# One new order for all operations of an attention and feed-forward kernel

## The chip, the cores and the metric

The program runs on one NeuronCore of a Trainium2 chip. The metric is the device time of one execution in microseconds, lower is better; the time of a kernel is the median of its runs. A profile is one further execution, recorded by the hardware profiler, with a time of its own.

The core has five queues of instructions: PE (matrix products), DVE (element-wise work), ACT (element-wise work and functions such as exp), POOL (slower element-wise work) and SP (which here only starts transfers). Each takes its instructions strictly in order; an instruction that has to wait holds up all that stand behind it on the same engine. Transfers run on 16 DMA engines. In this kernel SP and ACT start them.

## The reference

```python
def rmsnorm(x, g):
    rms = np.sqrt(np.mean(x * x, axis=-1, keepdims=True) + 1e-06)
    return x / rms * g
# q, k, v: (8 batches, 12 heads, 448 positions, 64); float32
q_n, k_n = rmsnorm(q, g_q), rmsnorm(k, g_k)
attn = softmax(q_n @ k_n^T / sqrt(64))
x = (attn @ v), heads side by side             # 3584 x 768
out = ((x @ w_a) * (x @ w_b)) @ w_out           # 768 -> 1536 -> 768
```

The three weight matrices arrive as float64; all else is float32.

## The kernel before

**Two halves of work.** Attention goes over 24 groups `p` of four heads (three groups per batch, 8 batches). The feed-forward part goes over four pairs of batches, `beta` 0 to 3.

**Attention of one group.** SP loads q, k and v. ACT squares q and k (`squares`, L424), DVE adds the squares up (L426), POOL takes the power -1/2 (L432), DVE scales q (`apply`, qn, L436). PE transposes k and q (`transposes`, L462) and ACT copies both out of PSUM (qkT: L467 for k, L469 for q). For each of seven blocks `j`, PE makes the scores (`scores`, sc, L483), ACT the exponentials (ET, L489), PE the products with v (`values`, o, L505). The sums of the exponentials are made on PE with a matrix of ones for the first five groups (`sums_over_keys`, su, L541), later on DVE and POOL. Then `invert`: ACT copies the sums (rec, L554), SP spreads one row over many partitions (few, L561), DVE takes the reciprocal (L574), SP writes it to DRAM and reads it back to all partitions (L566, L570), DVE multiplies (`divide`, L612). The tiles that hold scores (tag `sc`) are two in number, so the third score product waits for the exponentials of the first.

**Weights.** 18 pieces of the weights are loaded by ACT's queue (`factors`, L347 and L350), split out of their 64-bit words by one ACT pass (Abs, L237, tile st) and six long DVE passes (L238 to L246), combined (L360) and written to DRAM (`keep`, L368 and L371) for later use. Two tiles st take turns, as do the places of the raw words (hraw, lraw).

**Feed-forward.** The products are made in seven instead of eight block products (`quarter_products`, L1168; `last_product`, L869); for `beta` 2 and 3 this is done twice over (`deep_products`, L745, in 42 steps (m, f) each, and `inner_products`, L1066). DVE and ACT add the partial results up (dt, dF). While attention lasts, these products fill PE where attention waits; afterwards PE has nothing else.

**The start.** PE also runs five groups of dummy products (`warm`, L1259) on a unit matrix, and one product that spreads the gains (pg, L1251).

**What sets the order.** Every operation is noted with `plan.op(engine, cost, key, emit, reads, writes, ...)`. `Plan.run` emits all 4367 operations in the order that the constant `ORDER` holds, and only asserts that the precedence derived from the names in `reads` and `writes` holds. So the order on every engine is that of `ORDER`. The costs, `kb` and the constants of `Plan` (`RATE`, `LANDING`) fed the search that made `ORDER`, which is not in the file; at run time they do nothing. Waits between engines are put in from the tiles that instructions really touch, not from these names. Some names stand for no data: `ffn` (all feed-forward products, in one sequence), `streaming`, `ended`, `quarter`, `firsts...`, `half...`, `at...` and others. They only held pieces of the order in place.

Of the kernel before, what the change touches and what calls it, by code (L numbers as in the profile page):

```python
# [19 lines left out]
def _float_of(bits):  # L20
# [6 lines left out]

ORDER = (
    "c-rk(30PEDmj3U3?^P95ul9va1q8L*rPZ`%qMdZRqsBExlWsd|1d&n^aAjXy;t~+|4MYox8>keZqKJYT7c?p^Xtp-vBxZBc^UZWVrzc<cH|M<q"
    "6iw1gGBaO)<GuB6-SzzEoO{nb=dz!Ol?d(%CmiMy7o1LKkke!`nXM+kYLbn{4MwBUWR#7o5ENv9za9ZjCp!8&GJC?_Bh@jgd(tQ@7&EdPhL0E?"  # L30
    "KWCj=a<dyV<J@uLmDn~zV#JtfQPG$RJ|#Olb4n&Zz66U=m6~-JnU&kNm7}<zumCIx3%70AwRiJo$eX~}cF)|6+qQAGc0F5*Kdr_$d8_}p{=u5H"
    "U&sGp74mYClarhC`<%DpI_$=l9b2Tko43KXEg#?|xV6c+>&EUi*VyWvz|J+0cI+rZ;f@@f>Ua9oe<J@_HEhTKeapXzVm0pL$QMgZ-b$1)Z#6r3"
    "{6N-`JNv7dv$VXiq7?9YuO2*zgJ-<jy%(_OT<QLj5@tV!lYg{!Kl}i^i2p|gDu6@xD{-Lw(*s`|EIWw(`}bQ87nBxMVqe9+3Y2+kabS;B%1&CX"
    "5RQOyC97a{g~z>YoA=YQBebNlA1XeotT^yterefzD7k%L|IJdAmXuVH{;Mux7s~6s6<%*Z1?s$&-m)6g!Lnm(y=#x`_joQ<dP)RV;>EtQXZ~FB"
    "r+p>+N=r&h{;T8z&-?p4?e@I;?ycMJdKy2wb?;tdW8=Rxn(sE=YV>$+dWvsI#SIO`H__<6`Df2JSFd|K2d-ZBT)F7E^oL80^}#o9)z^D&G+g`S"
    ";~Uo-{`p$N9pm-iHC!ud@HAXGckasNx6U?rzG*1FQe6Lz$5Vf)?(N^#o%{0s&a+>fK2v+zbE)p~#rlsg)ycnmr+#PAyB99(tU2zfzE*v``ugdH"
    "+RInouKl{Mw)(=!qGKn%yze<vbK>~X@io;aPTaj)U32cZ=h&G$?;oquRGmImTUUF%uBx``L{-hn6E!topFe-HhU!&c{p+dw)u%qMEBdtd$R|fV"
    "HAkze&)uy)>+#4(58bZ94tP&q+g^e4V^`k6rNWC3P;lUU0rKD8hp)==w_+>XTyk&gC-*jgTxzpnBk<w6b;XRmw|&!^by&R)Se>^jZ&f{3t<1$&"
    "$axcQuCxQomH}_DB@8fRXW>0$W*{RS>1jx3wq#1c!eqXH&&PZQLn0CrkPr{djzb)?+uXqP>6jkF7>kY~60c9el*yPp36o#5W8%b#z^^CrSNSU@"
    "K4Cl<#=V4>#sXtTV>B&(5g0aX_%O}^3?2jw9Do7+(Z3)1Gy4mafM2}8`|>{M^Bj?Wwl{kBf)3C0L{Db3bpyI|L6^>qhB|cwIz%8M9O3N|9%e^K"  # L40
    "NC?n2g!7LOWMl{oK!88|U4YX82gyul78Yh=%$Uux3=El>$j;EErz0aR9chi(%$9`|vbyB?NejW}&z-w8@l@vG%#(?U>FMc-8HqAO((I(9g-J^m"
    "vPF9qEX<0-ta(Lg3+B#Ey)u7p{;UNBbLP(jn}d__@p(XO4orL+qN3uWqG!&S8SRcv!}KV3Y)nj%J7$MryI-MUie8%Zx<)rC_P0{ZZ(^q97<5|c"
    "^_=mqj(>T=_;EV#xR+mf<&_C9j~%^m()_XWG-D=?8l}^W7&mtKOJj$P9rkL}*rB7O5hF&97&B^Y<jBb3BQ?W@R1VW(<j4_`BVHUjc-Y`Ukpl+~"
    "jvO>-@IcML0Rvu)j2s#nIY85Yh%|U0rG5j33>Y*>>fc5B)i3*L@T=#AUkH822%|^$9o0t?41zFpsO0B2SkekQ2%;dqAc;aBs?ZNy<eW2sPJqC`"
    "M8;`H1Z7JFGwnE(8mE4NnQ6$E{R8|tb24UkaN0>bXJ)f+K%v4!ZXp7cgO!5&2XO9kIs|TGR&IH8s)E7HO;dw~ARZVf5HHTA$<}7LZ<|VViLAh#"
    "%;_LJn2C4F3bzoMMO370BeV$?gOo)sn#>$_;<Oc2RpzFZED(V#fGSQpW)25~-R2vRWxbw3$Dx4)5lE5AqT)YG_-w&^8l8oNJ2Pj-&z?7%8nKw}"
    "j%{d&1^wP}V_H3MDGE^+K0p6<^d~sYP**nvuYEA7=Cu!xe=w;UxIxSwzIx>F<;ysP!-py>aTXQj73GJ@%PVS7Sq*P_dD%yI%TZYll<&V?Hij<p"
    "8~aDoZHiHQFQLBv;_eGx?0OMrN{fq2YWEeNI6-&q-h2D7kL}sLr>JP}E}(d4aq*5ljYT*1?7nt&$gV4%%S9euRJdb%QDNcvA=^<{TUc<SxBx}R"
    "J|B2==T46YJ9aQ^D%^zpg1z|#+c)NK-I`Cg)8#_GnQf~-U+{eX*|Qt5ar2fno7ST*)~#FBCpWK8?vdQw{Ic9lgEnuxy#Z|f?u{GPtzWreC6?!{"
    "S-m!I%ksRuRi_?otlO}$W<&qnb!%5u<*r>-nOl+j?5bsN<n&vyvftk4mhWD+j1}h;@65|tRKIf3n=4klxhQw#;^n;;EnT)^>C$D3a*izh^4W@&"  # L50
    "6|8*4l3oY1-&mZTm6f?PD<dPLSJqp-Gq-1^ZA&{}@LYa&YSwd$QZh1A($h0D($iBi4riw?OHcErBQ<q@_MJr~X<55dGt*L2(mcr-sYSh#lTuQW"
    "(ECirg5Ig~f1aG0lAQcZa{BV*Wj{|!PF}nOixPpXOw5^`mbf#qXwK|8NMQ4@m2S}u2??`PX0MqQ*Jb8>_X4*&C()hgj*oXIfX$jU3vo!AF>~fL"
    "_cV9HjCgl!e5Yu-dONzK-Lcc6W2VJUjh@=^bvAYC)G0HjxFcrFh>eYP$HvZ7iW!q*C&$FZOplq|VOn%F+b}O`ZbbU>@WhOWl*EL25#cGnj*DP)"
    "q0gNg78ai{b6ohW31Q>iVX?7c(bJ;Qo*^1hquRCu+O<I>g-8ep>dzoKT~74%cMNlaj<^$cSS;NvUGXe>TP-lsaW{97jrb`HojU1dy<$&VjgF2!"
    "Szvo8cLl5#b4N2Xt$oI1HCdF1jIvTu{=1oAqM*zOlPnu$GZmfHnyi*4xr<R9HdEwAecffHw`tUD?4k6UnkQT3pUGwmWtoUu%qDAhg0RRcm`u65"
    "*=*`%mdz%Wu!7c&%16<<K1%)}8hmg)jjiFj%N8qTi_K!O%4S;+vzb~1Z?>9MHhxCXvdX+lr<&kYkrmE~jM><g=<RA^=Sk_Fg!4&9<Yh|}oNTlx"
    "(y23PP8a#rhwOigbWiH?r_}y_xK_$EH7QfkVmH&1x_sYk`Zi^fusvFlul!y(xn=LD)~voo#;%YJFz5|>{X$u<G3dG6+0RdJ@YCu2bUM9G=Lap*"
    "b!1vetI=w>q~%&s5;UTu5j2u0YD7WO20@glLn0q0am7bjnT1JuSu%u3?ZVngZQFv*f7>?X7lQn89L{#mUd})#Ts;C@0Rb+Dzsu=zkaKc69Lfjs"
    "5iXa_=CJ+5X18@9cVU4gSfD*3NgQT4Y(}fqW-}UXwC|)uCbu=pZH(Zu!C;UDy;aZ5=%A0#>cU9?tyZViX*AGC8ZL_DcNv#C@ku@o#A+a?np1G9"
    "PSVW7eyJDefgvc<$SXas`a1H^^pVYJhPRibe+rdCB#E~P(FKcbOk$8I2D$<RT>h>A(dln=YMi}9(JoqTqS>k*E0OkBZ!vZ=nwWA>1VWefq+&l#"  # L60
    "+SM_gNZf^JL@g<k{Jz9G5F}}e`@B9e5y9BQCS3vT)!;!58OX!anlPx`(_9(}=bfpc#1722KtL#%TJyCzLZG_T=4N~Pd%)S(N}Y=xNlpqu_@^y^"
    ";qU<p5~%@P3g?PS6a}gbfQK=5+{a<1!a0O6v>+BM9W9U>n=pywLl%S%thI!#00m71m1@n`7U=>c0hI`ef(KQ8#?>0huTl@C(AG!3bF+w{Oyx)g"
# [1395 lines left out]
```

## Time and profile before

| | us |
|---|---|
| median of three runs | 1499.23 |
| the three runs | 1498.65, 1499.23, 1500.0 |
| profiled execution, its own time | 1502.8 |
| span of the instructions in it | 1500.9 |
| busy in it: PE, DVE, ACT, POOL | 1466.2, 1003.3, 438.8, 320.7 |
| moved by DMA | 250.75 MB, mean 167 GB/s |

The profiled execution is 3.6 us above the median of the runs, and 1.9 us of it lie outside the span. In the views below, an instruction row gives its start in the span, its duration, the engine, the line of the kernel, the operation, the tiles (result first), the shapes and a count; what stands in brackets is how long its engine sat idle just before, and what ended that idle time. Consecutive like instructions are merged into one row. PEq, ACTq and SPq are the sequencers: there a row is the issue of a transfer.

### The profile page before, as it was taken

How to read it: one execution, taken by the hardware profiler on the slowest of the kernel's cores; microseconds unless marked ns; L12 is line 12 of the kernel's file. 1: busy time of each engine (PE TensorE's matmuls, PEld its weight loads, DVE VectorE, ACT ScalarE, POOL GpSimd, SP SyncE). 2: the span in 40 equal slices, each digit the busy share in tenths (PEclk: the TensorE clock that was granted, in tenths of full speed). 3: DMA queues.
4: the chain of work that ended last, by engine and by line, in shares of the span. 5: the costliest groups of instructions: out<-in, count | busy, mean ns of one | idle time of the engine just before them, and what ended most of it. 6: DMA issues, size and time to landing. Idle time of an engine off the chain costs nothing.

```text
span 1500.9 us, 21032 instructions
## 1 busy us (share of the span) xinstructions
PE 1466.2 (98%) x7854; PEld 957.4 (64%) x7854; DVE 1003.3 (67%) x1568; ACT 438.8 (29%) x790; POOL 320.7 (21%) x172
## 2 busy tenths in 40 slices
PE   8988999999999999999999999999999999999998
PEld 5333344555444555555544445699998899999798
DVE  5786869888875333334577766477787677777785
ACT  5766772111454000000167771011111011111000
POOL 3324543111343000101166641011210001121000
PEclk9999999999999999999999999999999999999999
DMA  9888545555342455445667544655555765554554
GB/s 252 242 247 232 123 100 186 179 179 212 122 119 90 141 154 181 143 152 159 192 172 175 133 129 124 189 165 158 158 158 170 246 194 163 158 158 133 171 193 134
DMA packets 189075, 250.75 MB, mean 167 GB/s; under 512 B 61988, under 2 KB 160804, under 8 KB 182308
## 3 DMA queue, kind: packets, MB, share of 16 engines
q1 hardware_dynamic: 160900, 195.82, 45.6%
q10 hardware_dynamic: 28064, 53.48, 10.4%
q8 instruction: 65, 1.06, 0.3%
q14 instruction: 46, 0.38, 0.1%
HBM read 191.10 MB, written 57.97 MB: 166 GB/s over the span
## 4 chain that ended last, share of the span: by engine, by line
PE 87%; DMA 5%; DVE 4%; ACT 2%; SPq 1%; issue 1%; POOL 0%; ACTq 0%; DVEq 0%; POOLq 0%
PE pq L1168 25%; PE dg L745 17%; PE po L869 16%; PE da L745 6%; PE sc L483 6%; PE o L505 6%; PE g L1066 2%; PE a L1066 2%; PE pt L462 2%; DMA k_sb<-in_k_dram 1%; PE b L1066 1%; PE e L1066 1%; PE d L1066 1%; DMA few<-rec 1%; PE su L541 1%; ACT ET L489 1%
## 5 line engine op out<-in xcount | busy, mean ns | idle before, releaser
L1168 PE MATMUL pq<-x,st 128*128 128x448 f32 x1008 | 382.6, 540 | 0.5 <-DVE hT L1203 0.3
L1168 PEld LDWEIGHTS pq<-x,st 128*128 128x128 f32 x1008 | 190.3, 190 | 189.5 <-issue 178.8
L489 ACT ACTIVATE ET<-sc,ms 128x448 f32<-128x448 f32 x336 | 190.8, 636 | 66.9 <-PE sc L483 52.6
L432 POOL TENSOR_TENSOR ms<-ms,expo 128x14 f32<-128x14 f32 x48 | 144.6, 3016 | 168.3 <-DVE ms L430 168.1
L745 PE MATMUL dg<-dT,st 128*128 128x224 f32 x672 | 168.7, 354 | 1.6 <-DVE dt L785 1.6
L745 PE MATMUL dg<-x,st 128*128 128x224 f32 x672 | 168.8, 353 | 0.2 <-DVE dF L792 0.2
L483 PE MATMUL sc<-qkT 64*64 64x448 f32 x1344 | 154.7, 545 | 14.2 <-ACT qkT L469 6.9
L869 PE MATMUL po<-st,hT 128*128 128x384 f32 x492 | 163.5, 488 | 0.0
L505 PE MATMUL o<-ET,v_sb 64*64 64x448 f32 x1344 | 150.4, 540 | 2.1 <-ACT ET L489 2.1
L773 POOL TENSOR_TENSOR hT<-dF 128x448 f32<-128x448 f32 x42 | 47.3, 1139 | 424.6 <-DVE dF L768 423.5
L869 PEld LDWEIGHTS po<-st,hT 128*128 128x128 f32 x492 | 92.6, 190 | 65.6 <-issue 5.7
L745 PEld LDWEIGHTS dg<-dT,st 128*128 128x128 f32 x672 | 126.4, 190 | 4.0 <-DVE dt L785 3.6
L745 PEld LDWEIGHTS dg<-x,st 128*128 128x128 f32 x672 | 126.6, 190 | 2.5 <-DVE dF L792 1.7
L745 PE MATMUL da<-x,st 128*128 128x224 f32 x504 | 123.1, 353 | 0.9 <-ACT dt L758 0.9
L483 PEld LDWEIGHTS sc<-qkT 64*64 64x64 f32 x1344 | 46.6, 132 | 99.5 <-ACT ET L489 40.4
L519 POOL TENSOR_TENSOR sum<-sum,ET 128x896 f32<-128x896 f32 x38 | 82.0, 2159 | 113.7 <-DVE sum L519 52.7
L505 PEld LDWEIGHTS o<-ET,v_sb 64*64 64x64 f32 x1344 | 51.4, 133 | 75.8 <-issue 62.7
L768 DVE TENSOR_TENSOR dF<-dF 128x896 f32<-128x896 f32 x84 | 95.5, 1137 | 2.3
L745 PEld LDWEIGHTS da<-x,st 128*128 128x128 f32 x504 | 92.9, 189 | 4.4 <-ACT dt L758 1.9
L758 ACT COPY dt<-da 128x224 f32<-128x224 f32 x84 | 29.1, 346 | 213.9 <-PE da L745 200.2
L869 PE MATMUL po<-st,fin 128*128 128x384 f32 x252 | 86.6, 491 | 0.0
L1216 POOL TENSOR_TENSOR hT<-hT,t 128x448 f32<-128x448 f32 x12 | 14.4, 1200 | 325.1 <-DVE t L1214 325.1
(136 smaller groups left out, 1719.6 us busy)
## 6 DMA issues: line engine op xcount, KB each, us to landing
st<-kept_o SPq DMA_DIRECT2D x28, 1152.0 KB
st<-kept_s SPq DMA_DIRECT2D x84, 320.0 KB
kept<-st ACTq DMA_DIRECT2D x12, 1344.0 KB
st<-kept SPq DMA_DIRECT2D x12, 1344.0 KB
st<-kept SPq DMA_DIRECT2D x84, 192.0 KB
ti<-kept_t SPq DMA_DIRECT2D x48, 288.0 KB
kept_s<-ds SPq DMA_DIRECT2D x30, 448.0 KB
q_sb<-in_q_dram SPq DMA_DIRECT2D x48, 224.0 KB
```

What stands on the lines that cost most here:

```text
L432: lambda: nc.gpsimd.tensor_tensor(msf(), msf(), expo[:, 0:2 * NT * (b - a)], ALU.pow), [], names)
L462: nc.tensor.transpose(t[:, j * P:(j + 1) * P], x[:, j].rearrange("p h d -> p (h d)"), ident)
L483: nc.tensor.matmul(t[low_high[w], e, 0:S], lhsT=qkTs[p][low_high[e], 1, j * P + w * D:j * P + (w + 1) * D], rhs=qkTs[p][low_high[e], 0, w ...
L489: nc.scalar.activation(E[:, e], scs[p, j][:, e, 0:S], AF.Exp, scale=rs[p][:, 1, 2 * j + e:2 * j + e + 1])
L505: nc.tensor.matmul(os_[p][low_high[e], w, 0:S], lhsT=xs["v", p][low_high[w], e, j * D:(j + 1) * D], rhs=ETs[p, j][low_high[w], e], start=( ...
L519: two[e].tensor_tensor(sums[p], sums[p] if j > 1 else ETs[p, 0], ETs[p, j], ALU.add)
L745: nc.tensor.matmul(to(), lhsT=W(w), rhs=t(), start=not more and k == 0, stop=k == len(terms) - 1, skip_group_check=True)
L768: take("DVE", 1.09, lambda: V.tensor_tensor(F[to], F[to], F[other], ALU.add), allF(other), allF(to), lock=True)
L773: lambda: two[e].tensor_tensor(C(i, n), F[g][:, 0:S], F[g][:, S:2 * S], ALU.mult), allF(g),
L869: nc.tensor.matmul(held["po"][:, 0:HALF], lhsT=a[0]()[:, c], rhs=sts[beta, 12 + place_of[f]][:, c], start=(c == 0), stop=(c == MH - 1))
L1066: nc.tensor.matmul(held[bank], lhsT=x()[:, c], rhs=y(c), start=(start and c == 0), stop=(stop and c == MI - 1), skip_group_check=True)
L1168: nc.tensor.matmul(banks[bank][:, 0:S], lhsT=sts[at][:, f, c * P:(c + 1) * P], rhs=quads[x][:, c], start=(start and c == 0), stop=(stop an ...
```

## The change

The order is made anew. Nothing is added or removed among the instructions; every operation keeps its engine, its tiles and its size. What changes in the file:

- `ORDER`, a new constant.
- Names that match `HINT` are dropped from `reads` and `writes` before precedence is derived, so ten kinds of precedence that no data need are gone. Counted over all operations, 18678 precedences become 17481.
- The costs that the search used for transfers: `LANDING` from 1.85 to 1.65, and `kb` by kind (some up, some down). The change describes its search as one over five cases in which transfers come late.

```diff
+HINT = re.compile(r"ffn|ended|held|streaming|quarter|deep factors|inner (factors|sums)|at\d+\.\d+|half-?\d+|firsts\d+")
...
 ORDER = (
-    "c-rk(30PEDmj3U3?^P95ul9va1q8L*rPZ`%qMdZRqsBExlWsd|1d&n^aAjXy;t~+|4MYox8>keZqKJYT7c?p^Xtp-vBxZBc^UZWVrzc<cH|M<q"
...
+    "c-rk(33OFulCJ;1>wE9+_r4`BJ4tY13kWE-Vk_=Mzy(Feg+K^|5JDoDg@lB#h!ROcSYk+k7ZAt-gzS(7hD~J+C`N^LVRUq`J$;<<X!jXCGj&5)"
...
-    RATE, LANDING = 310.0, 1.85
+    RATE, LANDING = 310.0, 1.65
...
         n, deps, tiles = len(self.ops), set(), set()
+        reads, writes = ([x for x in names if not HINT.fullmatch(x)] for names in (reads, writes))
...
-                op(LOADS, 0.4, key - 0.75, load, after, [f"{row}/{part}"], kb=768)
+                op(LOADS, 0.4, key - 0.75, load, after, [f"{row}/{part}"], kb=690 if last else 860)
...
-            op(KEEPS, 0.45, key, keep, [f"{st}/{x}" for x in range(7)], [f"kept{n}"], kb=1376)
+            op(KEEPS, 0.45, key, keep, [f"{st}/{x}" for x in range(7)], [f"kept{n}"], kb=1000)
...
-               kb=460 if nm != "k" else 800, dmas=2)
+               kb={"q": 690, "k": 770, "v": 530}[nm], dmas=2)
...
-            op("SP", 1.65, p - 0.0, spread_out, [t], [few], new=[few], kb=20, dmas=2)
+            op("SP", 1.65, p - 0.0, spread_out, [t], [few], new=[few], kb=8, dmas=2)
...
-            op("SP", 1.22, p - 0.0, come_back, [f"inv{p}"], [t], kb=460, dmas=2)
+            op("SP", 1.22, p - 0.0, come_back, [f"inv{p}"], [t], kb=710, dmas=2)
...
```

How the order moves, counted in operations: 944 of the 1450 on PE change place, half of all by one place or less and none by more than 15; on DVE 1138 of 1566, on ACT 357 of 678, on POOL 54 of 164, on SP 325 of 455. The places that the prediction speaks of:

- Start, PE: all five `warm` groups, then pg, then the transposes of k and q of group 0. Before: two `warm` groups, k, pg, two `warm`, q, two score products, the fifth `warm`. Start, ACT: the first three weight loads stand before and after the squares of k; before they stood behind the copy of the gains or later.
- Group 3, ACT: the copy of q (L469) now stands ahead of the weight load that stood before it. The load, another one and the Abs of the next piece now stand ahead of the first exponentials of group 3.
- `invert`, DVE: the reciprocal of group 1 stands one long DVE pass later; that of group 2 one pass earlier, but its transfers are issued earlier (ahead of q of group 5 on SP, and ACT copies the sums ahead of two other copies); that of group 3 behind three more operations.
- Group 2: PE makes the scores in the order 1, 2, 0, and the products with v of block 0 stand directly behind the scores of block 0.
- `deep_products`: where every step had the same pattern, the steps are now interleaved in many patterns.

## The prediction

> **What bounds the kernel now.** I read the busy shares first, then the same by stage, then the waits and rows of PE.
>
> ```profile
> span 1500.9 us, 21032 instructions
> PE 1466.2 (98%) x7854; PEld 957.4 (64%) x7854; DVE 1003.3 (67%) x1568; ACT 438.8 (29%) x790; POOL 320.7 (21%) x172
> ```
>
> PE is busy for 1466.2 of 1500.9 us. Since no instruction is added or removed, an order can only win the other 34.7 us, and what PE loses to slow clock or changes of mode. Where they are, by stage (columns: stretch, its length, busy PE, PEld, DVE, ACT, POOL, granted clock, DMA share, GB/s):
>
> ```profile
> 0.00:25.00 25.00, 18.53 (x124) 13.34 (x128) 7.91 (x12) 12.18 (x17) 6.00 (x10) 0.86 0.97 232
> ...
> 75.00:100.00 25.00, 19.63 (x196) 7.17 (x189) 21.97 (x28) 15.29 (x23) 8.05 (x3) 1.00 0.79 212
> 100.00:125.00 25.00, 21.59 (x205) 10.68 (x205) 19.82 (x24) 16.39 (x26) 4.39 (x2) 1.00 1.05 303
> ...
> 200.00:950.00 750.00, 748.65 (x3512) 373.17 (x3511) 468.22 (x631) 232.42 (x377) 192.04 (x94) 1.00 0.51 153
> 950.00:1500.90 550.90, 541.92 (x2800) 504.65 (x2798) 388.14 (x759) 68.57 (x197) 47.34 (x42) 1.00 0.55 170
> ```
>
> In the first 25 us PE lacks 6.5 us, from 25 to 200 us 17.9 (5.4 and 3.4 of it in the two stretches shown), from 200 to 950 us 1.3, and in the last stretch 9.0, of which some 6 are the end after the last product (1494.7), which no order removes. So this is a change to the first 200 us, where no engine is full: PE waits there for chains through ACT and DVE, and these for transfers.
>
> **The start.**
>
> ```profile
> 1.36 3.50 PE L1259 MATMUL warm<-ident 128*128 128x128 f32 x16 [1.36 <-POOL ident masks.py:199]
> 7.93 1.73 PE L462 MATMUL pt<-ident,k_sb 128*128 128x128 f32 x7 [3.07 <-DMA k_sb<-in_k_dram]
> ...
> 10.10 3.79 PE L1259 MATMUL warm<-ident 128*128 128x128 f32 x16
> 13.68 1.42 PE L462 MATMUL pt<-ident,qn 128*128 128x128 f32 x7
> 16.25 1.74 PE L483 MATMUL sc<-qkT 64*64 64x448 f32 x16 [1.16 <-ACT qkT L469]
> ```
> ```profile
> 10.38 1.09 DVE L436 TENSOR_TENSOR qn<-q_sb,ms 128x896 f32<-128x896 f32 x1 [0.20 <-POOL ms L432]
> ```
>
> qn is ready at 11.47, but the transpose of q starts at 13.68, because dummy products stand ahead of it: 2.2 us. The new order runs all dummies first. They end at about 7.3 (14 at 0.213 us each, 26 at 0.111, the spacings in the first row before and after the clock rises), within the wait for k. Then pg waits for the gains (DVE is done with them at 8.42 in this trace), k follows, then q at 11.5. Scores start at 11.5 + 0.9 + 1.2 (from the end of the transpose, 15.1, to the scores) = 13.6 instead of 16.25: 2.6 us.
>
> *The clock.* The row: after 3.1 us without work the same transpose of seven blocks took 1.73 us, against 0.98 later; the clock had fallen back. The Trainium skill, "TensorE: Matmul & The Clock Gate", Part 1, says that the gate closes after an idle window of about 3.4 us, in windows that run freely, and opens after a busy one. In the new order no gap reaches 3 us (about 1.2 before pg, 1.9 before q, 1.2 before the scores), so by the rule the clock stays full and the gain is 2.6. But the row shows a fall after a gap shorter than the rule's window, and the new gaps together leave PE two thirds idle. If it falls, q costs 0.5 more and the first two score products about 1.5 more: the gain is 0.6. I take 2.2, nearer to the rule, since each gap is well under the one that the row shows. The three weight loads that now go out early add 0.3 to 0.6 us each to ACT's queue, while ACT waits for k (7.90); if they delay k by up to 1 us, qn, which stands behind k's sums on DVE, is late by as much; the low end covers that. Downstream ACT meets the same wait for the first weights at the next step (they landed at 19.65, 8.4 us after the second issue); issued 2 to 4 us earlier, they keep pace with the earlier start.
>
> **The block on ACT at 80 us.**
>
> ```profile
> 79.78 0.41 ACTq L350 DMA_DIRECT2D lraw<-in_moe_w_a_dram  x1
> 80.23 1.01 ACT L469 ACTIVATE qkT<-pt,gain 128x896 f32<-128x896 f32 x1 [5.67 <-DVE st L246]
> ```
> ```profile
> 81.30 1.74 PE L483 MATMUL sc<-qkT 64*64 64x448 f32 x16 [3.74 <-ACT qkT L469]
> ```
>
> A weight load waits for its buffer (DVE's last pass over the piece in it, L246, done at 79.75) and holds the copy of q behind it for 5.67 us; PE waits 3.74 us. The new order puts the copy first. That is not worth 3.74: the load, a second one and the next Abs (0.41, 0.58, 1.65 us) now stand ahead of the exponentials. PE has the scores and four sum or value products of 0.75 us first, then needs the exponentials for its third score product. With L246 about 1 us earlier (next paragraph) I get 78.8 + 0.5 + 1.65 + two blocks of 1.16 = 83.3 for that product, against 84.39 in the trace: 1.1 us, between 0 and 3.
>
> **The reciprocals on DVE.**
>
> ```profile
> 71.32 0.25 DVE L574 RECIPROCAL few<-few 112x16 f32<-112x16 f32 x1 [3.03 <-DMA few<-rec]
> 94.86 0.25 DVE L574 RECIPROCAL few<-few 112x16 f32<-112x16 f32 x1 [2.72 <-DMA few<-rec]
> 119.48 0.25 DVE L574 RECIPROCAL few<-few 112x16 f32<-112x16 f32 x1 [2.62 <-DMA few<-rec]
> ```
>
> Groups 1, 2 and 3: DVE stands still for 8.4 us in all because 3.5 KB take 5 to 6 us (6.15, 5.10, 6.23 in the chain of waits). Behind it wait the weight passes and the sums for the next q and k. In the new order group 1 gains one pass (0.9 us) of cover; this is the 1 us used above. Group 2 loses a pass but its transfer is issued at least one q load (1.77) and two ACT copies (1.0) earlier; group 3 gets a long pass, a sum of squares and a combination more ahead of it, 1.76 + 1.08 + 0.56 = 3.4 us against the 2.62 waited. PE's own waits downstream of these two are 0.93 and 0.63 (at 87 and 97 us) and 1.64 and 0.59 (at 125 and 127, where ACT stood behind DVE's sum for 2.48 us). Of the first I take 1.0, of the second 1.8: together 2.8 us, between 0 and 3.8.
>
> **What stays.** PE's 1.34 us at 116 comes from ACT standing 3.11 us for a piece whose tile was freed by a store of 13.0 us at a DMA share of 1.05; the piece has the same PE work ahead of it (7.6 us of products) in both orders. The 1.19 us at 142, behind a q load of 8.8 us: the exponentials are now ahead of that wait, the copy of q still behind it. I count both at nothing.
>
> **The start of the deep products.**
>
> ```profile
> 963.65 1.02 PE L745 MATMUL da<-x,st 128*128 128x224 f32 x4 [0.43 <-ACT dt L758]
> ...
> 967.15 0.65 PE L745 MATMUL dg<-dT,st 128*128 128x224 f32 x2 [0.96 <-DVE dt L785]
> ```
>
> At beta 2 the second part of da followed the first at once, though ACT must copy in between; now dg stands between, and at beta 3 a product of the next step (0.43 there too). With half of the 0.96 that is 1.2 us, between 0.4 and 2.0.
>
> **Changes of mode.** Between products of 64x64 and of 128x128 PE loses time: v products x16, 1.50 us alone, take 1.62 before a transpose, and the transpose 0.91 instead of 0.82. The new order has 90 such changes, not 96: 3 pairs of 0.2 us, 0.6 us.
>
> **Costs.** The scores of group 2 in the order 1, 2, 0 leave nothing between the scores of block 0 and its v product, while ACT needs 1.16 us for the exponentials and has the squares of k ahead of them: a new stall of 1.5 us near 60 us. The small waits not yet counted (15 from 39 to 176 us, 7.1 us in all) are mostly ACT's pace with two score tiles; the new order moves them, and I credit 1.5 us. In the deep steps the row of before is free of idle with 1.89 us of products between dg and the one that needs DVE's dF; now 7 of 84 have 1.14 or less, 14 have 1.5, and the rest as much or more. DVE's part is 0.62 us and the handing over, so I charge 0.5 us. In the copy by ACT nothing falls below the 0.76 us that sufficed, save one at 0.38. Elsewhere PE had no idle and the order changes little; moved loads on SP (v of group 15 some 45 places earlier, others by under 15) meet a DMA share of 0.5 and PE waits for no load after the start: nothing, between -1 and +2. On SP the q load of group 5 falls behind the transfers of group 2's sums, but has 7.6 us of products ahead of its squares instead of 5.3. On POOL sums (2.16 us) and powers (3.0) change places with a neighbour; POOL is busy for at most 16.6 of 25 us in any stretch: nothing, within 0.5.
>
> **Sum.** 2.2 + 1.1 + 2.8 + 1.2 + 0.6 + 1.5 - 1.5 - 0.5 = 7.4 us. The profiled execution would go from 1502.8 to 1495.4. It was 3.6 us above the median 1499.2, so the median becomes 1491.8.
>
> **Rivals.**
> - *Stalls only move.* In attention ACT and the transfers set the pace: in 150 to 175 us ACT is busy for 21.2 of 25, from 100 to 125 DMA is full. Then the gains of 1.1, 2.8 and 1.5 turn up as other waits of the same length, and 2.2 + 1.2 + 0.6 less half a microsecond is left: 3.5, so 1495.7, with cases up to no gain at all. For it: a stall of 3.74 us that yields 1.1 when followed up. Against it: DVE is idle for transfers at known places, and these get cover.
> - *Earlier weights carry.* Weights that go out 4 us sooner bring the whole preparation forward, so that feed-forward work to fill PE is there earlier: half of the 17.9 us from 25 to 200 goes, with the start and the deep part 13 us: 1486.
> - *Deep steps lose the beat* (slower). 21 of 84 steps now have less cover for dF than the 1.89 us that never stalled. If DVE has one of its wide additions (1.14 us) ahead when such a step comes, it is 0.2 + 1.1 + 0.6 = 1.9 after dg, and PE waits 0.4 to 0.8 us. At 0.6 in all 21 that is 12.6 us, so 1491.8 + 12.6 = 1504.4. It decides at 0.5 each (10.4 us: from 7.4 faster to 3 slower). Against it: in this stage DVE is busy for 17 to 18 of 25 us and itself waits for PE before dF (66 times, 43.9 us in all).
> - That the change does nothing: the order does change on every engine, so no.
>
> **How the numbers follow.** A measurement of this kernel can tell about 0.2% (3 us) from no change, so faster means under 1496.2. Forecast 0.62, all of it faster; stalls only move 0.25, of which 0.17 faster and 0.08 same; earlier weights 0.07, faster; deep steps 0.06, slower. That gives 0.86, 0.08 and 0.06. The range goes from 1485, near the case of earlier weights and the upper ends of the single gains, to 1498, which takes in most of the case in which stalls only move.
>
> **What would show it.** Right: the first score product at 13.5 to 14.5 us; no wait of over 1.5 us for qkT near 80; the reciprocals of groups 2 and 3 without idle of over 1 us; PE idle in the span down from 34.7 to about 28; the deep products without 0.43 at their start. Wrong: dummy or first score products at half speed after 11 us; PE's idle time from 25 to 200 us still near 18 under other names; rows of dg with idle of 0.3 us or more, many times, after 970 us; PE waiting for a load.

## The result, and the profile after

The changed kernel takes 1483.4 us (median of six runs, 1483.1 to 1489.5) against 1499.6 for the kernel before (median of six, 1498.2 to 1501.0): a ratio of 0.9899, with a 95% interval of 0.9883 to 0.9916. That is 16.2 us faster where 7.4 were forecast and 1485 was the lower end of the range. The direction was right, the size less than half. The profiled execution of the changed kernel took 1483.15 us, 1481.3 of it the span. Lines of the program stand ten later than before (L462 is now L472, L745 is L755).

From its page, the counterpart of the first two lines shown of before:

```profile
span 1481.3 us, 20985 instructions
PE 1460.9 (99%) x7854; PEld 957.9 (65%) x7854; DVE 983.6 (66%) x1568; ACT 437.3 (30%) x790; POOL 320.6 (22%) x172
```

The span fell by 19.6 us. (The profiled execution of before was 3.2 us above its median, so this is more than the 16.2.) PE's idle time, span less busy, fell from 34.7 to 20.4 us: 14.3. The other 5.3 us came out of *busy* PE, 1466.2 to 1460.9, although the products are the same. The prediction had a place only for slow clock and changes of mode there, and took 0.6 us for the latter.

By stage (stretch, its length, busy PE, PEld, DVE, ACT, POOL, granted clock, DMA share, GB/s):

```profile
0.00:25.00 25.00, 20.05 (x129) 13.47 (x133) 9.37 (x14) 12.21 (x17) 6.00 (x10) 0.86 0.99 252
25.00:200.00 175.00, 166.44 (x1487) 70.04 (x1483) 138.78 (x173) 131.84 (x210) 77.68 (x29) 0.99 0.78 210
75.00:100.00 25.00, 23.16 (x214) 10.28 (x210) 23.15 (x30) 17.85 (x28) 8.38 (x3) 0.93 1.02 272
200.00:950.00 750.00, 749.07 (x3487) 375.08 (x3480) 462.81 (x632) 225.57 (x366) 188.62 (x92) 1.00 0.52 156
950.00:1481.30 531.30, 525.29 (x2761) 499.35 (x2759) 372.64 (x751) 67.63 (x197) 48.30 (x42) 1.00 0.56 171
```

From 25 to 200 us PE's idle time is 8.6 us, where it was 17.9: 9.3 of the 14.3 us that went. In the last stretch 3.0 us went and in the first 1.5. The 6.0 us that are left in the last row lie behind the last product, as before.

The start, rows of PE and ACT:

```profile
11.70 0.98 PE L472 MATMUL pt<-ident,qn 128*128 128x128 f32 x7 [1.68 <-DVE qn L446]
12.17 0.34 ACTq L357 DMA_DIRECT2D lraw<-in_moe_w_out_dram  x1
12.55 0.16 ACT L1264 COPY gain<-pg 128x1 f32<-128x1 f32 x1 [3.55 <-DMA hraw<-in_moe_w_out_dram]
14.48 3.27 PE L493 MATMUL sc<-qkT 64*64 64x448 f32 x16 [1.79 <-ACT qkT L479]
```

The transpose of q starts 2.0 us earlier and the first score product 1.8 us earlier than before. But the scores take 3.27 us where they took 1.74: half clock. The kernel before had a stretch of half clock too, equally long, but it lay over the transposes of k, dummy products and part of the transposes of q:

```profile
7.84:14.66 6.82, 6.73 (x30) 6.41 (x31) 3.04 (x7) 2.02 (x3) 5.06 (x2) 0.50 0.93 265
```

And the third of the early weight loads, the ACTq row, goes out only at 12.17; the copies of gain, k and q queue behind it. It does not wait for its buffer. In the packed trace the transfers of SP and ACT count their landings on eight semaphores in all, and a transfer that reuses one waits until the earlier transfer on it has landed. The third load reuses the semaphore of the first (issued at 5.51, landed at 12.15). So the program has waits of this kind besides those that come from tiles.

The block near 80 us and the three reciprocals:

```profile
73.50 0.98 PE L493 MATMUL sc<-qkT 64*64 64x448 f32 x8 [0.18 <-ACT qkT L479]
79.59 0.98 PE L493 MATMUL sc<-qkT 64*64 64x448 f32 x8 [1.34 <-ACT ET L499]
```
```profile
68.33 0.25 DVE L584 RECIPROCAL few<-few 112x16 f32<-112x16 f32 x1 [3.19 <-DMA few<-rec]
88.84 0.25 DVE L584 RECIPROCAL few<-few 112x16 f32<-112x16 f32 x1 [1.55 <-DMA few<-rec]
113.35 0.25 DVE L584 RECIPROCAL few<-few 112x16 f32<-112x16 f32 x1 [1.05 <-DMA few<-rec]
```

The wait of 3.74 us for qkT became 0.18, and 1.34 for the exponentials behind the Abs. DVE's waits went from 8.4 to 5.8 us in all, the first of them not at all.

### Waits that PE's rows do not show

From 940 us to the last product, before had 2.7 us of idle PE and after has none; yet after wins more than that there. The list of PE's waits of before in that stretch (instruction, what it waited for, us in total, times, longest):

```profile
PE dg L745 <- DVE dt L785: 1.6, 3, 1.0
PE da L745 <- ACT dt L758: 0.9, 2, 0.4
PE dg L745 <- DVE dF L792: 0.2, 1, 0.2
```

And PEld's, the weight loads that go ahead of each product, of before and then of after:

```profile
PEld dg L745 <- DVE dt L785: 3.6, 7, 1.3
PEld da L745 <- ACT dt L758: 1.9, 3, 0.8
PEld g L1066 <- DVE oi L1122: 1.8, 8, 0.2
PEld dg L745 <- DVE dF L792: 1.7, 6, 0.5
PEld g L1066 <- DVE fin L1122: 1.4, 6, 0.2
PEld b L1066 <- DVE o_sb L892: 0.4, 1, 0.4
```
```profile
PEld dg L755 <- DVE dF L802: 1.3, 5, 0.4
PEld g L1076 <- DVE oi L1132: 0.7, 3, 0.2
PEld da L755 <- ACT dt L768: 0.7, 2, 0.4
PEld dg L755 <- DVE dt L795: 0.4, 2, 0.2
PEld a L1076 <- DVE pi L1111: 0.2, 1, 0.2
PEld dg L755 <- DVE dt L794: 0.2, 1, 0.2
```

10.8 us of waits against 3.5. (A wait of PEld need not cost PE as much, so these sums say where to look, not what is lost.) PE's record cannot show the short ones: a product dg or da is recorded as 0.35 us long and the next follows 0.19 us later, so a wait of up to 0.16 us lies inside the recorded span and counts as busy. The Trainium skill, "Perfetto Trace Analysis", Identifying the Most-Contended Engine, says that matmul busy time is no good measure of how close PE is to its limit, because matmuls are pipelined, and points to the share of the peak rate that is reached and to the weight loads' busy share. This case agrees with the first: PE is 98% busy in before, and 99% in a kernel 16 us faster. The weight loads' share tells little here (64 and 65%), but their *waits* tell it.

From here on I therefore measure PE by starts: each product has a usual distance to the next (0.094 us for scores, values and sums, 0.111 transposes, 0.376 pq, 0.323 po, 0.189 dg and da, 0.163 the inner products), 1421.9 us in all. What a stretch takes beyond that I call its loss; it holds idle time, hidden waits, slow clock and changes of mode. Loss in us by stretch of PE work, in the profiled executions:

```
                  0-12  12-105  105-160  160-870  870-1421   sum
before            17.3    25.0      7.1     14.6       8.8  72.7
before_again      16.4    24.7      6.5     14.9       8.8  71.2
inner_new         15.8    24.0      7.6     13.5       6.5  67.5
tail_new          15.5    22.5      7.5     13.5       2.1  61.2
tail_old          16.4    17.7      7.6     12.9       8.9  63.5
attention_new     16.3    16.5      7.7     16.4       8.8  65.7
stretch_new       15.3    14.0     10.2     13.9       8.9  62.2
pe_act_new        15.6    22.4     11.0     13.5       8.9  71.5
dve_sp_new        14.6    28.9      5.8     13.7       8.8  71.8
after             16.8    13.9      7.6     12.9       2.1  53.4
after_again       15.9    14.2      7.6     12.9       2.1  52.7
```

12 us of PE work end at about 29 us of time, 105 at about 147, 160 at about 209, 870 at about 934 (in the trace of before). The two columns in the middle of the attention and at the end hold the result: 12 to 105, and 870 to 1421. The last column repeats to 0.1 us between executions of one order (after_again's with after's, before_again's with before's). The first two scatter: after and tail_old have the same order in 12 to 105 and lost 13.9 and 17.7.

### The profile page after: what moved, and what is told of

Its sections match the earlier page's. It is cut to its first block, busy times and chain, and to the rows that moved or that the text cites. A ratio compares the mean times of both kernels' runs of the same rounds, so it can differ in the third digit from the quotient of the medians.

```text
span 1481.3 us, 20985 instructions
## 1 busy us (share of the span) xinstructions
PE 1460.9 (99%) x7854; PEld 957.9 (65%) x7854; DVE 983.6 (66%) x1568; ACT 437.3 (30%) x790; POOL 320.6 (22%) x172
## 4 chain that ended last, share of the span: by engine, by line
PE 88%; ACT 1%; DVE 1%; issue 0%; DMA 0%; SPq 0%; DVEq 0%; ACTq 0%
PE pq L1178 25%; PE dg L755 17%; PE po L879 16%; PE da L755 6%; PE sc L493 6%; PE o L515 6%; PE a L1076 2%; PE g L1076 2%; PE pt L472 2%; PE e L1076 1%; PE d L1076 1%; PE b L1076 1%; PE su L551 1%; DMA q_sb<-in_q_dram 0%; ACT ET L499 0%
## 5 line engine op out<-in xcount | busy, mean ns | idle before, releaser
L755 PE MATMUL dg<-dT,st 128*128 128x224 f32 x672 | 168.7, 353 | 0.0
L493 PE MATMUL sc<-qkT 64*64 64x448 f32 x1344 | 159.8, 552 | 7.0 <-ACT ET L499 4.2
L755 PE MATMUL dg<-x,st 128*128 128x224 f32 x672 | 164.9, 353 | 0.0
L755 PEld LDWEIGHTS dg<-dT,st 128*128 128x128 f32 x672 | 126.8, 190 | 1.3 <-DVE dt L795 0.4
L755 PEld LDWEIGHTS dg<-x,st 128*128 128x128 f32 x672 | 126.5, 190 | 1.7 <-DVE dF L802 1.3
L755 PE MATMUL da<-x,st 128*128 128x224 f32 x504 | 118.5, 353 | 0.1
L755 PEld LDWEIGHTS da<-x,st 128*128 128x128 f32 x504 | 94.5, 190 | 1.5 <-ACT dt L768 0.7
L778 DVE TENSOR_TENSOR dF<-dF 128x896 f32<-128x896 f32 x84 | 92.5, 1105 | 2.7 <-DVE dF L807 0.5
```

The costliest lines, as they stand in the source:

```text
L493: nc.tensor.matmul(t[low_high[w], e, 0:S], lhsT=qkTs[p][low_high[e], 1, j * P + w * D:j * P + (w + 1) * D], rhs=qkTs[p][low_high[e], 0, w ...
L755: nc.tensor.matmul(to(), lhsT=W(w), rhs=t(), start=not more and k == 0, stop=k == len(terms) - 1, skip_group_check=True)
L778: take("DVE", 1.09, lambda: V.tensor_tensor(F[to], F[to], F[other], ALU.add), allF(other), allF(to), lock=True)
```

## The experiments

Every kernel below is one of the two with part of the order exchanged; nothing is left out of the computation. In the edits `before[:n]` means the first n operations of that order, and names stand for operations. The kernel before ran beside each group (medians 1498.2 to 1499.2 us).

### How far before repeats

The edit: none.

> The kernel before, once more, unchanged. It shows how far the places of waiting repeat from one profiled execution to the next, and where the 3.2 us lie by which the first profiled execution of before (1502.8 us) was above its median (1499.6). If the waits of the first 200 us depend on when transfers land, they differ by 1 us or more here; those after 940 us depend on PE and DVE alone and should repeat within 0.5 us.

It took 1501.27 us. Loss by stretch as in the table: ahead of 160 us of work 1.8 us less than the first execution, the last column the same. So the slow part of the profiled executions lies in the first 200 us, and the end can be compared to a tenth of a microsecond.

### The end: deep and inner stages

```diff
-before
+before[:2404] + [x for x in after if x not in before[:2404]]      # tail_new
-before
+before, its operations 3136 to 3342 and 4043 to the end in the sequence of after      # inner_new
-after
+after[:2433] + [x for x in before if x not in after[:2433]]       # tail_old
```

> The old order up to 940 us (2404 operations), then the new one: only the two deep stages, the inner products and the last products are changed. Idle only (the premise of the prediction: what PE can win is what its rows show as idle): before has 2.7 us of idle there ahead of its last product and after none, so 2.7 us faster, about 1496.9. Pace (a wait of less than about 0.16 us hides in the recorded spans, which are 0.35 us for products that follow each other every 0.19 us): by start-to-start spacing above the usual pace before loses 9.1 us there and after 2.5, so 6.6 us faster, about 1493. Lost beat (the rival of the prediction): slower than 1499.6.

1491.76 us, ratio 0.9962 (0.9948 to 0.9975): 3.7 to 7.8 us faster. In the trace the last column goes from 8.8 to 2.1: 6.7.

> The old order with the new one only in the two stretches of inner products (between the deep stages, and after the second). Idle only: before has not one row of idle of PE there, so no gain, 1499.6. Pace: before starts 28 products of g some 0.1 us late (14 after e, 14 after g), after only 7 of them; with the few others 2.4 us faster, about 1497.2.

1497.04 us, ratio 0.9990 (0.9982 to 0.9997): 0.4 to 2.7 us faster. In the trace 2.3 us (8.8 to 6.5); of the 28 late products of g (14 behind e, 14 behind g) 7 are left. Before, an inner group looked like this:

```profile
1159.89 1.14 PE L1066 MATMUL g<-ti,Si 128*128 128x192 f32 x6
1160.87 1.14 PE L1066 MATMUL e<-st,Si 128*128 128x192 f32 x6
1161.53 0.35 DVE L1122 TENSOR_TENSOR fin<-pi,g 128x192 f32<-128x192 f32 x1
1161.94 0.95 PEld L1066 LDWEIGHTS g<-ti,fin 128*128 128x128 f32 x6 [0.23 <-DVE fin L1122]
1161.94 1.24 PE L1066 MATMUL g<-ti,fin 128*128 128x192 f32 x6
```

The second g reuses the place of the first, which DVE must have read (fin, done at 1161.88). It starts 1.07 us behind e instead of 0.98, and its own first product is followed late too, so that six take 1.24 instead of 1.14. No row of PE has a bracket. In inner_new other products stand between:

```profile
1158.21 1.14 PE L1071 MATMUL e<-st,Si 128*128 128x192 f32 x6
1159.19 4.03 PE L874 MATMUL po<-st,hT 128*128 128x384 f32 x12
1163.06 1.14 PE L1071 MATMUL g<-ti,fin 128*128 128x192 f32 x6
```

> The kernel after up to the start of the deep products (2433 operations, about 945 us), then the old order. The counterpart of tail_new: what it loses against after is the worth of the new order in the deep and inner stages. Pace: 6.6 us slower than after, 1490.0. Idle only: 2.7 us, 1486.1. Its gain over before is that of the first 945 us, cleanly cut: 9.3 us by the first, 13 by the second.

1490.96 us, ratio 0.9943 (0.9929 to 0.9957), 7.6 us slower than after. By pace 1490.0 was expected, by idle rows alone 1486.1. So the deep and inner stages give some 6.7 us of the 16, from both sides; 2.7 of it showed as idle time of PE in before, and about 4 was hidden.

### The attention stage, taken whole

```diff
-before
+after[:685] + [x for x in before if x not in after[:685]]
```

> The new order for the first 685 operations (in the trace of after, up to about 200 us), then the old order for all the rest. By the idle time of PE alone: the first 200 us lacked 24.4 us in before and 13.5 in after, so 10.9 us faster, about 1488.7. By the lead of after in the same PE work (12.6 us at 240 us, of which up to 3.2 may belong to the slow profiled execution of before): 9.4 to 12.6 us faster. If the old order of the feed-forward part was made for the old landing times and gives part back: 6 to 8 us faster, about 1492.5.

1495.69 us, ratio 0.9978 (0.9969 to 0.9986): only 3.1 us. The table shows two reasons. From 160 us of work on it loses 16.4, some 2.5 more than the old order and 3.5 more than the new: behind the seam the old order waits, first 1.14 us at 208 us for a qkT. And in 12 to 105 this execution lost 16.5 where after lost 14. So this run says little about the worth of the attention stage; tail_old, cut at a calmer place, says it better: the new order up to 945 us is 7.6 us faster than before, where 9.3 to 13 were expected.

### The terms of the forecast, done alone in before

```diff
 # ACT, group 3 (copy_first)
-load lraw/1/0
 copy of q (qkT3)
+load lraw/1/0
 Abs of piece 14
```
```diff
 # DVE (recip_later); SP's write behind groups 2 and 3 moves along
-reciprocal of group 1
 long pass of piece 12
+reciprocal of group 1
...
-reciprocal of group 2
 last long pass and a combination of piece 14
+reciprocal of group 2
...
-reciprocal of group 3
 last long pass of piece 1, sum of squares of k
+reciprocal of group 3
```

> The kernel before, with a single change: the weight load that holds ACT for 5.67 us at 74 to 80 us stands behind the copy of q of group 3 instead of ahead of it. By the prediction's term: the load now holds the Abs and the exponentials behind it, so of PE's 3.74 us only 1.1 is won, about 1497.7. If the exponentials are not held (PE has enough other work): 3.7 us faster, about 1495.1. If the stall only moves: 0, about 1498.8.

1499.82 us, ratio 1.0010 (1.0001 to 1.0019): nothing won. The wait for qkT is gone; in its place:

```profile
77.15 1.61 ACT L241 ACTIVATE st<-lraw 128x1536 f32<-128x1536 f32 x1 [4.55 <-DVE st L250]
78.66 2.18 ACT L493 ACTIVATE ET<-sc,ms 128x448 f32<-128x448 f32 x4
79.85 2.57 PE L487 MATMUL sc<-qkT 64*64 64x448 f32 x16 [2.16 <-ACT ET L493]
121.21 5.04 PE L487 MATMUL sc<-qkT 64*64 64x448 f32 x32 [1.93 <-ACT qkT L473]
```

ACT still stands, one place later, until DVE's pass (st, L250 there) frees the buffer; the Abs and then the exponentials are late, and PE waits 2.16 us for these.

> The kernel before, with only DVE's reciprocals of groups 1, 2 and 3 (and SP's write that follows each of the last two) moved: group 1 behind one long pass (0.96 us), group 2 behind the last long pass and a combination of the piece (1.76 + 0.56), group 3 behind the last long pass and the sum of squares of k (1.76 + 1.08). DVE waited 3.03, 2.72 and 2.62 us there. By the prediction's term: 2.8 us faster, about 1496.0. If these waits are the cause of all that the new order wins between 88 and 125 us (2.0 + 3.2 us in the two stretches of PE work, beyond the usual pace): 5 us faster, about 1493.8. If the sums that come back later hold up the divisions and with them the next groups: 0, about 1498.8.

1500.03 us, ratio 1.0009 (1.0000 to 1.0018): nothing won. DVE's waits did shrink, from 8.4 to 3.2 us (2.52, 0.70, none). But the sums come back later, and ACT waits for divisions by them:

```profile
106.84 0.97 ACT L558 COPY rec<-su 128x448 f32<-128x448 f32 x2 [2.19 <-DVE x L616]
108.39 1.12 PE L509 MATMUL o<-ET,v_sb 64*64 64x448 f32 x5 [1.94 <-ACT ET L493]
```

### By engine

```diff
 # operations 85 to 470 of before, about 25 to 146 us
-PE, ACT in the sequence of before
+PE, ACT in the sequence of after          # pe_act_new
-DVE, SP, POOL in the sequence of before
+DVE, SP, POOL in the sequence of after    # dve_sp_new
-all engines in the sequence of before
+all engines in the sequence of after      # stretch_new (78 to 470)
```

> The kernel before, with the new order of PE and ACT alone in the stretch from 25 to about 146 us (operations 85 to 470); DVE, SP and POOL keep the old one. In that stretch the old order loses 22.5 to 25 us against the usual pace of PE, the new one 13.9 to 16.6. If the gain is the hand-over between PE and ACT (which score product, which exponentials, which copy comes first: many waits of 0.3 to 1.0 us): 6 to 9 us faster, about 1491. If it is the transfers and DVE's waits for them: at most 2 us. If it needs both: at most 2 us here and in dve_sp_new.

1500.03 us, ratio 1.0002 (0.9993 to 1.0012).

> The complement: the kernel before, with the new order of DVE and SP (POOL's is the same) alone in the same stretch; PE and ACT keep the old one. It takes in all moves of the reciprocals, of the sums of squares, of the weight passes and of the loads. If DVE's waits are the cause of the gain: 5 us faster or more, about 1493. If it is the hand-over between PE and ACT: 0 to 2 us. If it needs both: at most 2 us in either.

1500.24 us, ratio 1.0008 (1.0001 to 1.0014). What each half runs into, ACT of pe_act_new and then of dve_sp_new:

```profile
78.33 1.60 ACT L241 ACTIVATE st<-lraw 128x1536 f32<-128x1536 f32 x1 [5.01 <-DVE st L364]
119.29 0.95 ACT L428 ACTIVATE sq<-q_sb 128x896 f32<-128x896 f32 x1 [3.87 <-DVE ms L430]
```
```profile
42.84 2.21 ACT L493 ACTIVATE ET<-sc,ms 128x448 f32<-128x448 f32 x4 [3.08 <-DVE st L364]
98.51 0.95 ACT L428 ACTIVATE sq<-q_sb 128x896 f32<-128x896 f32 x1 [5.18 <-DVE ms L430]
```

ACT in the new sequence asks for a free buffer or a finished sum before DVE in the old sequence is there, and the other way round.

> The kernel before, with the new order of all engines together in the stretch of pe_act_new and dve_sp_new (operations 78 to 470, about 24 to 146 us). Those two gave +0.9 and +1.1 us. If the gain of the attention stage belongs to no single engine but to orders that fit one another: 6 to 9 us faster, about 1491.5. If it comes from the first 24 us (the earlier weight loads, say), which stay old here: at most 2 us, about 1498.

1493.40 us, ratio 0.9972 (0.9963 to 0.9981): 5.2 us faster by the medians (2.8 to 5.5 by the interval) where 6 to 9 were expected; neither of its halves was faster (0.9 and 1.1 us slower by the medians). In the stretch itself the loss is 14.0, as low as in after, against some 24 with the old order. 3 us are given back behind the seam (105 to 160: 10.2 against 7.2), where ACT waits 3.44 us for a q load and PE 3.71 us behind it. The trace shows no late issue: the load went out at 134.99, 1.0 us behind a weight load, and had landed at 143.31; in after its counterpart takes from 136.81 to 141.26, and the weight load goes out behind it. Whether the weight load slowed it is not shown. So the gain of this stretch belongs to neither pair of engines and to none of the single moves tried; it needs PE and ACT on the one side and DVE and SP on the other in sequences that match. What SP's nine moved operations do in it was not tried alone.

### The same terms, undone in after

```diff
 # ACT, group 3 (copy_old)
+load lraw/1/0
 copy of q (qkT3)
-load lraw/1/0
```
```diff
 # DVE (recip_old); SP's write behind group 3 moves along
+reciprocal of group 1
 long pass of piece 12
...
-reciprocal of group 1
...
+reciprocal of group 3
 last long pass of piece 1, sum of squares of k, a combination of piece 0
-reciprocal of group 3
```

> The kernel after, with one single move undone: the weight load of group 3 stands ahead of the copy of q again, as in before. In before the move alone gave nothing (copy_first). If its worth only shows where the rest is new: slower than after, by 1.1 to 3.7 us (1484.4 to 1487). In after DVE's pass that frees the buffer (L256) ended at 75.8 and the copy was done at 73.45, so the copy would come 3.3 us later. If another wait takes its place either way: as after, 1483.3.

1484.84 us, ratio 0.9907 (0.9892 to 0.9922), 1.6 us above after_again, whose interval overlaps with it. PE waits 3.47 us for qkT again, but the 1.34 us for the exponentials and 0.49 us behind them are gone: 1.6 net. But the profiled execution lost no more from 12 to 105 than that of after (13.8 against 13.9), so a cost of undoing this move is not shown.

> The kernel after, with DVE's reciprocals of groups 1 and 3 back in their old places (ahead of the first long pass over st12; ahead of the last pass over st1, with SP's write behind it). Moved alone in before they gave nothing (recip_later). If they are worth something where the rest is new: 1 to 3 us slower than after (DVE waits again 0.9 us for group 1 and 2.6 for group 3), 1484.3 to 1486.3. If DVE's wait has cover in PE's work either way: as after, 1483.3.

1486.47 us, ratio 0.9918 (0.9903 to 0.9934), 3.2 us above after_again (the intervals overlap by a little). The profiled execution lost 16.4 us from 12 to 105, 2.5 more than after. DVE waits 3.05 and 2.58 us for groups 1 and 3 again, and PE has in exchange:

```profile
69.03 0.98 PE L492 MATMUL sc<-qkT 64*64 64x448 f32 x8 [2.76 <-ACT qkT L476]
116.34 1.74 PE L492 MATMUL sc<-qkT 64*64 64x448 f32 x16 [2.49 <-ACT qkT L478]
```

So the later reciprocals, worth nothing alone in the old order, are probably worth some 2 to 3 us where the rest is new. The forecast's 2.8 was for groups 2 and 3, this run moves 1 and 3, so the sizes can't be compared. For the copy of q nothing is shown.

### The start and the weights

```diff
 # ACT, group 0 (start_load; load_and_abs as well)
-load lraw/0/0
 copies of gain, k, q
+load lraw/0/0
 # PE (start_warm, on top of it)
-warm, warm, warm, warm, warm, pg, transposes of k, of q, scores
+warm, warm, warm, pg, transposes of k, warm, transposes of q, warm, scores
 # ACT, group 3 (load_and_abs, on top of start_load)
-Abs of piece 14
 exponentials of block 1
+Abs of piece 14
```

> The kernel after, unchanged, beside the next three on the same chip. About 1483.4; it shows how much a second profiled execution of it differs in the first 150 us (the first one lost 12.1 + 5.8 us up to the twelfth us of PE work, then 13.9 us up to the 105th), and whether start_load (1486.25) was really slower than after or only measured apart from it.

1483.25 us, ratio 0.9896 (0.9884 to 0.9909).

> The kernel after, with one operation moved: ACT's third weight load stands behind the copy of q (qkT) of group 0 instead of ahead of the copy of the gains. In after this load was issued at 12.17 us, and the copies behind it could only begin at 12.55. Without it the copy of k needs only pt (10.02), so the copy of q begins at 12.75 and the first scores at 13.85 instead of 14.48. If the slow first scores (x16 in 3.27 us instead of 1.74) come from the wait of 1.79 us ahead of them, they run at full clock now: 0.6 + 1.5 + about 0.8 in the next products = 2.9 us faster than after, about 1480.5. If PE was already too thinly busy from 8.6 us on (two transposes of 0.98 us in 5 us), the clock still falls: 0.6 us faster, about 1482.8.

1486.25 us, ratio 0.9922 (0.9909 to 0.9936), 3 us slower than after, although its profiled execution was one of the three fastest of all runs here (1480.94). In that one the copies are free at once, but PE runs at half clock all the same, and from the transposes of q on:

```profile
11.46 1.75 PE L471 MATMUL pt<-ident,qn 128*128 128x128 f32 x7 [1.29 <-DVE qn L445]
14.37 3.27 PE L492 MATMUL sc<-qkT 64*64 64x448 f32 x16 [1.16 <-ACT qkT L478]
```

> The same, and two of the five groups of dummy products (8 each, 0.9 us at full clock) are moved from the front: one behind the transposes of k, one behind those of q, where PE has nothing to do. If the clock falls for want of work between 8.6 and 14.5 us, it stays full here: first scores at 13.9 in 1.74 us, 2.9 us faster than after, about 1480.5. If the clock's fall does not depend on that, as start_load or slower than it by up to 0.4 where a dummy group ends after qn or the copy of q. If an early gain is lost again by the end of attention: within 1 us of after.

1485.57 us, ratio 0.9924 (0.9901 to 0.9947). The first scores do run at full clock now (1.73 us), but the clock was low from 8.5 to 15.3 us instead: the transposes of k took 1.76, a dummy group 1.92, and the scores began only at 15.71. The fewer dummies at the front left 2.85 us empty ahead of pg.

> The kernel after with two single moves: the one of start_load, and at 77 us the Abs (1.66 us) behind the first exponentials of group 3 instead of ahead of them, since PE waits 1.34 us there for them (at 79.59) while DVE takes up the Abs only at 79.87, 1.4 us after it is done. If both waits are real and nothing takes their place: 0.6 to 2.4 us by the first and 1.1 by the second faster than after_again, about 1480.5. If the profiled execution of start_load was merely a lucky one: as after_again or up to 1 us faster.

1486.62 us, ratio 0.9919 (0.9905 to 0.9933): 3.4 us slower than after_again, on the same chip. The Abs moved its wait once more: 0.17 us for the exponentials at 78.60 instead of 1.34, but 2.01 at 81.59, where ACT is late with the copies of the sums (rec) instead of 0.49. Why the kernels with the later third load are slower in most executions (start_load 1485.6 to 1488.0 in five of six) stays open; the profiled executions, 1480.9 and 1484.2, are among their fast ones and do not show it.

```diff
 # ACT: three weight loads (weights_old on after; weights_new the reverse on before)
-squares q, load, squares k, load, load, copies of gain, k, q
+squares q, squares k, copy of gain, load, load, copies of k, q, exponentials, load
```

> The kernel after, with the first three weight loads on ACT put back: two behind the copy of the gains, the third behind the first three pairs of exponentials of group 0, as in before. Earlier weights carry (the rival of the prediction): most of the 9 us of the attention stage is lost again, 1488 or more. If the early loads matter little: within 1 us of after, 1483.3; as the third load no longer holds the copies of k and q at 12.2 us, up to 1 us faster. start_load, which delays one of them by 1.2 us, was 3 us slower than after though its profiled execution was 2.2 us faster; if the landing of the first piece sets a pattern for the next 100 us, this one is slower by 3 us or more too.

1481.87 us, ratio 0.9885 (0.9868 to 0.9901). Not slower but, if anything, 1.4 us faster than after_again; it has the lowest median of all, though its interval overlaps with that of after.

> The counterpart: the kernel before, with only the first three weight loads issued early, behind the squares of q and k of group 0 as in after. Earlier weights carry: 4 us faster or more, 1494.5 or less. If the gain of the attention stage is that all engines' orders fit one another: 0 to 1 us faster, about 1498.5; where the third load holds the copies at 12 us as in after, up to 1 us slower.

1500.08 us, ratio 1.0003 (0.9993 to 1.0012). The three early weight loads alone carry nothing.

## Why the prediction was right and wrong

The table sets each part of the forecast beside the difference of mean losses between executions with the old and with the new order in that stretch. The executions are these:

- Start: the eight whose first 78 operations or more are those of before, without stretch_new and weights_new (14.6 to 17.3), against the six with the start of after (14.9 to 16.8). Four of them are not in the table of losses: copy_first and recip_later lost 15.3 and 14.8, copy_old and recip_old 16.3 and 14.9.
- Second row, 12 to 105: before, before_again, inner_new and tail_new against after, after_again, attention_new and tail_old.
- Third row: 105 to 160 of the same eight, and 160 to 870 of those with the old order in it except attention_new (13.5 to 14.9), against 12.9.
- The end: as in the table of losses.

| step | forecast | measured |
|---|---|---|
| start | 2.2 | -0.4 (15.7 to 16.1) |
| ACT block 1.1, reciprocals 2.8, small waits +1.5 and -1.5 | 3.9 | 8.5 (24.1 to 15.6) |
| changes of mode, the middle | 0.6 | 0.6 (21.1 to 20.5) |
| deep products 1.2 - 0.5 | 0.7 | 6.7 (8.8 to 2.1) |
| sum | 7.4 | 15.4 (medians: 16.2) |

**The first claim failed.** "An order can only win the other 34.7 us, and what PE loses to slow clock or changes of mode" left out waits that count as busy. In the deep and inner stages 0.7 us was forecast and 6.7 measured: 2.7 that the rows show as idle, of which the forecast took 1.2, and about 4 that they hide. This is the largest miss, 6 us, and the view that shows the hidden part, the waits of PEld, was there in the trace of before. "The row of before is free of idle" was taken as proof that 1.89 us of cover suffices in the deep steps; it was not. The list of PEld's waits of before has six for dF.

**The start gave nothing** (0.4 us worse, within the scatter). The first score product came at 14.48, just inside the 13.5 to 14.5 named as right (16.25 before). But the clock fell, which the prediction named as the other case (0.6 us) and set aside because no gap would reach 3 us. None did; the longest was 1.8 us. In 3.4 us of the start of after (first row) PE worked for 0.98, and the clock was halved in the next 6.8; at 81.83 us it fell again, after 3.4 us with 1.76 of work:

```profile
10.20:13.60 3.40, 0.98 (x7) 0.75 (x7) 1.48 (x4) 1.05 (x3) 2.87 (x2) 1.00 1.03 317
13.60:17.00 3.40, 2.52 (x16) 0.80 (x16) 0.00 (x0) 1.45 (x3) 0.00 (x0) 0.50 1.06 288
17.00:20.40 3.40, 3.40 (x20) 1.62 (x20) 1.31 (x2) 3.07 (x5) 0.00 (x0) 0.50 1.02 335
78.42:81.83 3.41, 1.76 (x14) 0.60 (x18) 3.38 (x6) 3.41 (x8) 2.45 (x1) 1.00 1.08 220
81.83:85.25 3.42, 3.42 (x24) 1.82 (x20) 3.38 (x3) 2.01 (x5) 0.00 (x0) 0.50 1.10 319
```

The length of the gaps was the wrong measure. In all 20 traces the granted clock changes only at points that lie whole multiples of 3.413 us apart, so a trace falls into windows of that length; where the windows lie differs between executions of one order (before has an edge at 4.42 us, before_again one at 14.04, which is not a whole number of windows later). The dummies of after ended at 8.64 instead of the 7.3 forecast, because its clock rose only at 6.74. Up to 1460 us, each of the 25 windows at full clock in which PE is recorded as busy for less than 1.40 us was followed by half clock; of the 18 with 1.40 to 1.77 us, 6 were; of the other 8400 or so, none. The idle window of the rule that the prediction took from the Trainium skill ("TensorE: Matmul & The Clock Gate", Part 1) thus need not be empty: here a window with less than 1.40 of 3.41 us of work acted as one.

Half speed cost 1.5 us in the scores and nearly as much in the sixteen products behind them (8 in 1.49 and 8 in 1.45 us from start to start, where 0.75 is usual); that is what the gain was spent on, and start_load and start_warm show the same fall at other places. The early loads, costed at 0.3 to 0.6 us of issue each, held ACT for 3.55 us, which the forecast did not see. For PE that was a small part: in after_again ACT is held for 3.34 us, and PE waits for the copy of q only 1.16 us, as in before.

**The attention stage was right in part and wrong in method.** Each term was costed alone, against the old order of all else. Alone, the two that were tried give nothing: "Stalls only move" was true of both. Together with the rest they give 8.5 us in this stretch, more than twice the sum. PE's waits from 25 to 200 us, 17.1 us in before and 8.3 in after, show where the sizes were off; they are matched by their place, in one execution of each. Near 80 us 3.74 became 0.18, 1.34 and 0.49: 1.7 won, where 1.1 was forecast. Of the 3.8 us behind the reciprocals about 3.4 went (2.8 forecast), although DVE's wait for group 1 stayed and those for groups 2 and 3 only shrank. The 1.34 us at 116 and the 1.19 at 142, both counted at nothing, went: 2.5 us, the largest miss here, and after_again has neither of them. Group 2's new order cost 1.1 (at 59.48) where 1.5 was charged, and the small waits fell from 7.1 to 4.8, 2.3 where 1.5 was credited. The forecast had no rival for moves that are worth more together.

**The middle agrees by chance.** Its 0.6 us is the sum of 0.4 lost from 105 to 160 and 1.0 won from 160 to 870; no run tells what changes of mode have to do with it.

**The rivals.** "Earlier weights carry" came nearest in its number (1486) and is refuted as a mechanism, for the three loads that go out early, by weights_new and weights_old. "Deep steps lose the beat": DVE's dF keeps dg waiting 1.3 us in all instead of 1.7; the price of 0.5 to 0.8 us at each thin place was not paid, and dt, which dominated, was relieved.

**Of what was to show it:** idle of PE fell below the 28 named, to 20.4; the reciprocals of groups 2 and 3 still show over 1 us; no load made PE wait; the deep products start without the 0.43. Of the signs of a wrong forecast only the half clock came.

## What to carry to other kernels

Look for a full engine's losses in its spacing and in its weight loads' waits, not in its idle time: where the recorded span of a product is longer than the distance to the next one, every wait shorter than the difference counts as busy. When two in-order engines hand buffers to each other, cost their orders together: a move that frees one of them is worth nothing until the other arrives earlier too, and undoing it in the new order tells more of what it is worth there. To keep the clock up, look at how much PE works in each few microseconds, not only at its longest gap. And judge by several executions: one order's first 147 us scattered by more than most of the edits gave.

## What the runs showed of the hardware

- The granted clock fell when PE had been busy for less than 1.40 of the 3.413 us of a window at full clock (25 of 25), and never above 1.77 us; in after it fell with no gap above 1.8 us.
- A wait that is shorter than a product's recorded span less its spacing (0.35 less 0.19 us for dg and da) does not show as idle time of PE: about 4 us of before's last 550 us.
- The same order repeats to 0.1 us in the last 550 us, but eight executions with the old start differ in their first 12 us of PE work by up to 2.7 us (losses of 14.6 to 17.3).
